# Reordering the opening of a fused retention and feed-forward kernel, with three units' outputs unfused and the last product split over two PSUM banks

## The chip, the core and the metric

The kernel runs on one core of a Trainium2 chip. The metric is the device time of one execution in microseconds (us); the figure given for a kernel is the median over its runs. TensorE (PE) does the matrix products, VectorE (DVE), ScalarE (ACT) and GpSimd (POOL) work beside it, each in the order of its own program; SyncE (SP), ScalarE and GpSimd also issue DMA transfers. The engines meet through semaphores. PSUM, where TensorE writes its results, has eight banks of 2 KB per partition.

## The reference

Multi-head retention (8 batches, 8 heads, 576 positions, head width 64) is followed by a two-layer feed-forward block over the 4608 resulting tokens:

```
scores = q @ k.T / 8                       # per batch and head, 576 x 576
ret    = scores * D                        # D[i,j] = gamma_h ** (i-j) for i >= j, else 0
x      = (ret @ v), heads side by side     # 4608 x 512
h      = x @ w_in                          # 512 -> 2048
g      = max(0.01 * h, h)                  # leaky ReLU
out    = g @ w_out                         # 2048 -> 512
```

Inputs and output are fp32; the kernel computes its products in fp16 with fp32 accumulation.

## The kernel before

**Retention by chunks.** The 4608 tokens are cut into 36 units of 128 tokens, each of two chunks of 64 tokens. Nine chunks make up one batch entry, so a unit can straddle two entries. Within a chunk the product q k^T v is done with a triangular mask; everything earlier in the entry comes through a running state, a 64 x 64 matrix for each head. The powers of gamma are folded into q and v by a table (`decay`), and the state is rescaled every four chunks.

For a unit u the steps are these; the names are those of the code.

- `load(u)` brings q, k and v (256 KB each) to SBUF. `cast_k`, `cast_q`, `cast_v` turn them into fp16; the last two also multiply by the table. For units 0 to 7 q and v are cast on VectorE and k on ScalarE.
- `transpose_pe(u, x)` turns k (x = 1) or q (x = 0) on TensorE into a PSUM bank, and `transposed` copies it out. From unit 8 on a DMA transposes instead (`transpose_dma`, issued on SP); `ahead(u)` issues the casts and that transpose.
- `scores(u)` is 32 matmuls into two PSUM banks: k^T q for both chunks, and each chunk's own contribution to the state.
- `state(u, j)` adds that contribution to the running state (VectorE; two operations where it is rescaled), `state_cast` makes an fp16 copy, `masks(u)` applies the triangle.
- `outputs(u)` is 32 matmuls that leave two separate parts in PSUM: what comes from the unit's own chunks and what comes from the state. `own(u)` (ScalarE) copies the first part to SBUF, and `add(u)` (VectorE) adds the second to it and writes x. `outputs_acc(u)` lets TensorE add both parts in PSUM, in two rounds with a drain between them, and `x_copy(u)` (ScalarE) writes x.

**Feed-forward by groups.** Four units make a group of 512 tokens. The first layer is computed in pieces: `h_half` (two blocks of 128 hidden features over two units), `h_unit` (four blocks over one unit), `h_block` (one block over a whole group); each is followed by a leaky ReLU on ScalarE (`leaky`, L387) into `gt`. `halves(g, (a, fb), ...)` calls `h_half` for token half a and feature pair fb. The second layer of group 0 is the plain product (`wide`); from group 1 on each group's second layer is done with seven half-size products in place of eight (`seven`), whose sums of inputs are prepared by `mix` and `mix_weights` on VectorE. `keep`, `give` and `store` combine the products and send them out. In the last group the final product p7 is added in two parts, so that each part can be stored by itself.

**PSUM.** The pool `sc` holds one buffer of two banks for scores, `ot` one buffer of two banks for outputs, and `acc` four single banks that rotate through everything else: turns, warm-up products, h pieces, second-layer products.

**What sets the order.** The order is written out by hand (`manual_schedule`): each engine runs its instructions in program order. Lines 560 to 621 are the opening, in which units 0 to 3 are done one after the other while the first weights arrive; `keep_warm(n)` puts n matmuls on zeros on TensorE there (L551). Lines 691 to 759 weave units 4 to 7 and the first-layer pieces of groups 0 and 1. `turn(u, x)` is a turn whose copy is on VectorE; `settle(u)` is state, cast, mask, state; `finish(u)` is `outputs_acc`, `x_copy` and a state cast on ScalarE; `finish2(u)` is `outputs`, `own`, `add`. Lines 766 to 798 hold the steady part.

The loads of the opening go out on three queues: SP has k of unit 0, half of q of unit 0, and k of unit 1; ScalarE's queue has two tables of constants and the other half of q of unit 0; GpSimd's queue has v of unit 0, then everything else of units 1 to 7 and all weights. The first layer's weights come in quarters of the hidden features, each in two transfers.

Of the kernel before, what the change touches and what calls it, by code (L numbers as in the profile page):

```python
# [9 lines left out]
FP = mybir.dt.float32  # L10
# [8 lines left out]
def kernel(  # L19
# [186 lines left out]
    def transposed(u, x, copy):  # L206
        copy(out=qkT[u][:, x], in_=tr[u, x])  # L207

    def scores(u):
        a = sc_pool.tile([P, 2, 2, NP, CH], FP, name="sc")  # L210
        sc_tiles[u] = a
# [96 lines left out]

    def outputs_acc(u):

        ot = ot_pool.tile([P, 2, 2 * NP, CH], FP, name="ot")
        ot_tiles[u] = ot
# [139 lines left out]
    def g_part(g, a, b):  # L452
        return g_t[g][:, b * HF : (b + 1) * HF, a * HT : (a + 1) * HT]
# [15 lines left out]
    def seven(g, hooks, last=False):  # L469
# [3 lines left out]

        def product(name, lhs, rhs, fresh):
            if fresh:
                r[name] = acc_pool.tile([P, 2, HN], FP, name="acc")
            order = (
                [(f, tb) for tb in range(2) for f in range(HF)]
                if last
                else [(f, tb) for f in range(HF) for tb in range(2)]  # L480
            )
            for n, (f, tb) in enumerate(order):
                nc.tensor.matmul(  # L483
                    out=r[name][:, tb, :],
                    lhsT=lhs[:, f, tb * P : (tb + 1) * P],
                    rhs=rhs[:, f, :],
                    start=fresh and n == 0,
                    stop=f == HF - 1,
                    skip_group_check=True,
                )  # L490

        def keep(name, of, plus=None):
            r[name] = m_pool.tile([P, 2, HN], FP, name=name)
            if plus is None:
                nc.scalar.copy(out=r[name], in_=r[of])
            else:
                nc.vector.tensor_tensor(out=r[name], in0=r[of], in1=r[plus], op=ADD)

        def give(a, b, of, plus=None, parts=1):
            if ("o", a) not in r:  # L500
                r["o", a] = o_pool.tile([P, 2, DM], FP, name="osb")
            for n in range(parts):
                ts = slice(n * 2 // parts, (n + 1) * 2 // parts)
                to = r["o", a][:, ts, b * HN : (b + 1) * HN]
                if plus is None:
                    nc.scalar.copy(out=to, in_=r[of][:, ts])
                else:
                    nc.vector.tensor_tensor(  # L508
                        out=to, in0=r[of][:, ts], in1=r[plus][:, ts], op=ADD
                    )  # L510
# [9 lines left out]
            if r["n", a] == 2 and not (last and a == 1):  # L520
# [8 lines left out]
            ("p5", g_part(g, 0, 0), w_part(1, 1), False, lambda: give(0, 1, "p5", "u2")),  # L529
            (  # L530
                "p7", g_part(g, 1, 1), w_mix[:, 3], False,
                lambda: give(1, 0, "p7", "u2", 2 if last else 1),
            ),
        )
# [25 lines left out]
    keep_warm(7)  # L560
    load(0, {1: nc.sync, 0: (nc.sync, nc.scalar), 2: nc.gpsimd})
    load(1, {1: nc.sync, 0: nc.gpsimd, 2: nc.gpsimd})
# [11 lines left out]


    cast_k(0)
    transpose_pe(0, 1)
    transposed(0, 1, act_copy)
    keep_warm(3)
    cast_q(0, nc.vector)  # L580
    cast_v(0, nc.vector)
    transpose_pe(0, 0)
    transposed(0, 0, act_copy)
    keep_warm(3)
    cast_k(1)
    for u in range(4):
        n = u + 1
        scores(u)
        if not u:
            keep_warm(3)  # L590
        state(u, 0)
        state_cast(u, dve_copy, (0,))
        masks(u)
        if not u:
            cast_q(1, nc.vector)
            cast_v(1, nc.vector)
        state(u, 1)
        if n < 4:
            transpose_pe(n, 1)
            transposed(n, 1, act_copy)  # L600
            if not u:
                keep_warm(3)
                outputs_acc(0)
                x_copy(0)
                keep_warm(1)
            transpose_pe(n, 0)
            transposed(n, 0, act_copy)
            keep_warm(3 if u else 2)
        if n < 3:
            cast_k(n + 1)  # L610
            cast_q(n + 1, nc.vector)
            cast_v(n + 1, nc.vector)
        if u < 3:
            state_cast(u, act_copy, (1,))
        if u == 1:
            outputs_acc(1)
            x_copy(1)
            keep_warm(2)
        elif u == 2:
            outputs_acc(2)  # L620
            x_copy(2)

# [67 lines left out]

    halves(0, (0, 0), (0, 1))
    finish2(3)
    state_cast(3, act_copy, (1,))
    halves(0, (0, 2), (0, 3), (1, 0))
    cast_k(4)
    cast_qv(4)
    halves(0, (1, 1))
    turn(4, 1)
# [17 lines left out]
    cast_k(6)  # L716
    cast_qv(6)
    halves(0, (0, 6), (0, 7))
    finish(5)
    halves(0, (1, 6))  # L720
# [3 lines left out]
    turn(6, 0)  # L724
    cast_qv(7)
    h_unit(5, 0)
    scores(6)
    settle(6)
    h_unit(5, 1)
    turn(7, 1)  # L730
    halves(1, (0, 4))
    finish(6)
    turn(7, 0)
    halves(1, (0, 5))
    scores(7)
    settle(7)
    load(8, after=(w_out_loads[2],))
    load(9)
    halves(1, (0, 6), (0, 7))
    h_unit(6, 0)  # L740
    finish(7)
    h_unit(6, 1)
    mix_weights(0, 0)
# [9 lines left out]
    mix_weights(2, 1)  # L753
    halves(1, (1, 5), (1, 6))
    load(11)
    ahead(9)
    mix_weights(3, 0)
# [71 lines left out]
```

## Time and profile before

| | |
|---|---|
| median of 7 runs | 294.23 us (291.59 to 295.34) |
| the profiled execution | 291.83 us |
| its span, first to last instruction | 290.1 us |
| TensorE busy, matmuls | 281.0 us (97%) |
| VectorE, ScalarE, GpSimd busy | 170.5, 144.3, 104.1 us |
| first h matmul (L373) starts | 19.11 us |
| warm-up matmuls (L551) | 30, busy 9.6 us |

The profile is of one execution. Its rows name the line, the engine, the operation, the tile that is written and the tiles that are read, with the number of instructions and their duration; in square brackets stands how long the engine had been idle before and what released it. Times in the timeline count from the span's start. Matmuls are pipelined: several overlap, so that a row's duration is longer than the distance between two starts. The time outside the span, 1.7 us in this execution, belongs to the measured time too.

### The profile page before, as it was taken

How to read it: one execution, taken by the hardware profiler on the slowest of the kernel's cores; microseconds unless marked ns; L12 is line 12 of the kernel's file. 1: busy time of each engine (PE TensorE's matmuls, PEld its weight loads, DVE VectorE, ACT ScalarE, POOL GpSimd, SP SyncE). 2: the span in 40 equal slices, each digit the busy share in tenths (PEclk: the TensorE clock that was granted, in tenths of full speed). 3: DMA queues.
4: the chain of work that ended last, by engine and by line, in shares of the span. 5: the costliest groups of instructions: out<-in, count | busy, mean ns of one | idle time of the engine just before them, and what ended most of it. 6: DMA issues, size and time to landing. Idle time of an engine off the chain costs nothing.

```text
span 290.1 us, 9449 instructions
## 1 busy us (share of the span) xinstructions
PE 281.0 (97%) x4118; PEld 191.2 (66%) x4118; DVE 170.5 (59%) x293; ACT 144.3 (50%) x254; POOL 104.1 (36%) x124
## 2 busy tenths in 40 slices
PE   6899999999999999999999999999999999999994
PEld 2468888745874587458745874588448844874583
DVE  1874577964762596359635862686268636841342
ACT  3666766724327732773277317731773176317510
POOL 8869601753433225222524342234225413000000
PEclk9999999999999999999999999999999999999999
DMA  7999999998999986966797669889986151012003
GB/s 199 303 226 198 295 206 208 224 231 177 239 217 293 210 186 156 280 149 147 159 251 174 148 147 277 159 127 168 272 167 144 42 180 38 5 66 81 0 2 145
DMA packets 131738, 50.01 MB, mean 172 GB/s; under 512 B 121264, under 2 KB 126000, under 8 KB 131696
## 3 DMA queue, kind: packets, MB, share of 16 engines
q1 hardware_dynamic: 124864, 39.46, 59.3%
q0 software_dynamic: 6016, 9.70, 14.9%
q8 instruction: 32, 0.52, 0.8%
q10 hardware_dynamic: 816, 0.24, 0.3%
q14 instruction: 10, 0.08, 0.1%
HBM read 36.81 MB, written 9.44 MB: 159 GB/s over the span
## 4 chain that ended last, share of the span: by engine, by line
PE 91%; DVE 3%; DMA 2%; ACT 1%; issue 1%; SPq 0%; DVEq 0%
PE acc L373 43%; PE acc L483 34%; PE acc L423 5%; PE sc L215 3%; DMA t<-in_k_dram 2%; PE ot L291 2%; PE sc L224 1%; PE ot L302 1%; PE ot L321 1%; PE acc L200 1%; DVE s L233 1%; ACT qkT L207 1%; PE ot L333 0%; ACT qk L172 0%; PE acc L551 0%
## 5 line engine op out<-in xcount | busy, mean ns | idle before, releaser
L373 PE MATMUL acc<-xT,w_in 128*128 128x512 f16 (+2 forms) x768 | 130.9, 326 | 0.0
L387 ACT ACTIVATE gt<-acc 128x512 f16<-128x512 f32 x144 | 85.9, 597 | 57.0 <-PE acc L373 55.5
L373 PEld LDWEIGHTS <-w_in 128*128 128x128 f16 x768 | 68.0, 98 | 51.5
L483 PEld LDWEIGHTS <-gt 128*128 128x128 f16 x640 | 61.7, 97 | 9.3
L233 DVE TENSOR_TENSOR s<-sc,cs 128x512 f16<-128x512 f32 x36 | 24.7, 686 | 40.8 <-PE sc L224 40.8
L273 POOL CAST st<-s 128x512 f16<-128x512 f32 x21 | 12.8, 609 | 93.5 <-DVE s L257 57.9
L483 PE MATMUL acc<-w_out,gt 128*128 128x256 f16 x384 | 45.9, 273 | 0.2
L355 ACT COPY own<-ot 128x512 f32<-128x512 f32 x30 | 17.6, 585 | 42.8 <-PE ot L302 35.2
L175 POOL TENSOR_TENSOR qk<-t,cs 128x512 f16<-128x512 f32 x28 | 30.4, 1087 | 15.7 <-ACT gt L387 14.5
L467 DVE TENSOR_TENSOR mix<-gt 128x1024 f16<-128x1024 f16 x16 | 14.7, 916 | 29.0 <-ACT gt L387 29.0
L179 POOL TENSOR_TENSOR v<-t,cs 128x512 f16<-128x512 f32 x28 | 31.3, 1118 | 0.5 <-PE acc L373 0.5
L483 PE MATMUL acc<-w_mix,gt 128*128 128x256 f16 x256 | 30.6, 273 | 0.0
L483 PE MATMUL acc<-w_mix,mix 128*128 128x256 f16 x256 | 29.5, 273 | 0.0
L483 PEld LDWEIGHTS <-mix 128*128 128x128 f16 x256 | 24.9, 98 | 3.2 <-DVE mix L467 0.2
L172 ACT CAST qk<-t 128x512 f16<-128x512 f32 x36 | 22.3, 620 | 1.8 <-DMA t<-in_k_dram 1.8
L360 DVE TENSOR_TENSOR xT<-ot,own 128x512 f16<-128x512 f32 x30 | 20.5, 683 | 3.0 <-ACT own L355 3.0
L257 DVE TENSOR_TENSOR s<-sc,s 128x256 f32<-128x256 f32 x40 | 16.8, 419 | 3.6 <-PE sc L224 3.1
L508 DVE TENSOR_TENSOR osb<-acc,u 128x512 f32<-128x512 f32 (+1 forms) x17 | 11.1, 656 | 8.0 <-PE acc L483 8.0
L215 PEld LDWEIGHTS <-qkT 64*64 64x64 f16 x576 | 7.7, 107 | 11.2 <-issue 9.7
L276 POOL CAST st<-s 128x256 f16<-128x256 f32 x7 | 3.2, 453 | 32.2 <-DVE s L261 20.3
L423 PE MATMUL acc<-w_out,gt 128*128 128x512 f16 x64 | 14.3, 380 | 0.0
L467 DVE TENSOR_TENSOR mix<-mix,gt 128x1024 f16<-128x1024 f16 x16 | 14.0, 879 | 0.5
(52 smaller groups left out, 238.4 us busy)
## 6 DMA issues: line engine op xcount, KB each, us to landing
out_dram<-osb SPq DMA_DIRECT2D x17, 512.0 KB, 3.8
t<-in_k_dram SPq DMA_DIRECT2D x27, 256.0 KB, 4.0
t<-in_q_dram SPq DMA_DIRECT2D x25, 256.0 KB, 4.5
t<-in_v_dram SPq DMA_DIRECT2D x25, 256.0 KB, 4.9
w_in<-in_moe_w_in_dram POOLq DMA_DIRECT2D x8, 256.0 KB, 7.3
w_out<-in_moe_w_out_dram POOLq DMA_DIRECT2D x4, 512.0 KB, 10.2
t<-in_v_dram POOLq DMA_DIRECT2D x7, 256.0 KB, 6.7
t<-in_q_dram POOLq DMA_DIRECT2D x6, 256.0 KB, 6.5
```

Source lines behind the costliest of these rows:

```text
L172: nc.scalar.copy(out=qk16[u][:, 1], in_=t32[u, 1])
L175: eng.tensor_tensor(out=qk16[u][:, 0], in0=t32[u, 0], in1=decay(u, 0), op=MUL)
L179: eng.tensor_tensor(out=v16[u], in0=t32[u, 2], in1=decay(u, 1), op=MUL)
L233: nc.vector.tensor_tensor(out=s16s[u], in0=sc_tiles[u][:, :, 0], in1=mask_sb.unsqueeze(1).unsqueeze(1).to_broadcast([P, 2, NP, CH]), op=MUL,)
L257: nc.vector.tensor_tensor(out=to, in0=st, in1=carry[0], op=ADD)
L355: nc.scalar.copy(out=owns[u], in_=ot_tiles[u][:, :, 0:NP].rearrange("q j c t -> q c j t"))
L360: nc.vector.tensor_tensor(out=x_of(u).rearrange("q (c g) t -> q c g t", g=2), in0=ot_tiles[u][:, :, NP : 2 * NP].rearrange("q g (c j) t -> ...
L373: nc.tensor.matmul(out=hps[:, n, :], lhsT=w_in16[:, c, f * P : (f + 1) * P], rhs=xT[g][:, c, ts], start=(c == 0), stop=(c == NP - 1),)
L387: nc.scalar.activation(out=out, in_=in_, func=mybir.ActivationFunctionType.Lrelu)
L423: nc.tensor.matmul(out=ys[tb], lhsT=g_t[0][:, f, tb * P : (tb + 1) * P], rhs=w_out16[:, f, :], start=(f == 0), stop=(f == NF - 1),)
L467: nc.vector.tensor_tensor(out=z[:, fs], in0=a[:, fs], in1=b[:, fs], op=op)
L483: nc.tensor.matmul(out=r[name][:, tb, :], lhsT=lhs[:, f, tb * P : (tb + 1) * P], rhs=rhs[:, f, :], start=fresh and n == 0, stop=f == HF - ...
```

## The change

**Opening.** It is written out step by step. Unit 0's q is loaded whole on SP's queue. The scores of units 0 and 2 go to the two banks of `ot` instead of those of `sc`, and the outputs of units 0 to 2 go to one bank of `acc`, so that the scores of unit u + 1 can be issued ahead of the outputs of unit u. The warm-up products are 23 instead of 30. The first h piece, `h_half(0, 0, 0)`, stands ahead of `masks(2)` and `scores(3)`.

**After the opening.** `cast_k(4)` and `cast_qv(4)` stand ahead of the h piece (1, 0).

**Units 5 to 7.** They use `outputs`, `own` and `add` in place of `outputs_acc` and `x_copy`. `cast_v(6)` moves behind the sum of unit 5, the casts of q and v of unit 7 move behind `settle(6)`, the sum of unit 6 moves behind the turn of unit 7's q, and unit 7's outputs move ahead of the h pieces (0, 6) and (0, 7) of group 1, which in turn move behind both `h_unit(6, ...)`. `ahead(9)` is issued before `load(11)`.

**The last product.** In the last group p7 lies in two banks, one for each half of its tokens, and each use of it is added and stored in two parts.

```diff
-    def scores(u):
-        a = sc_pool.tile([P, 2, 2, NP, CH], FP, name="sc")
+    def scores(u, pool=None):
+        if pool is None:
+            a = sc_pool.tile([P, 2, 2, NP, CH], FP, name="sc")
+        else:
+            a = pool.tile([P, 2, 2, NP, CH], FP, name="ot")
...
-    def outputs_acc(u):
-
-        ot = ot_pool.tile([P, 2, 2 * NP, CH], FP, name="ot")
+    def outputs_acc(u, pool=None):
+
+        if pool is None:
+            ot = ot_pool.tile([P, 2, 2 * NP, CH], FP, name="ot")
+        else:
+            ot = pool.tile([P, 1, 2 * NP, CH], FP, name="acc")
...
         def product(name, lhs, rhs, fresh):
+            apart = last and name == "p7"
             if fresh:
-                r[name] = acc_pool.tile([P, 2, HN], FP, name="acc")
+                r[name] = [
+                    acc_pool.tile([P, 1 if apart else 2, HN], FP, name="acc")
+                    for _ in range(2 if apart else 1)
+                ]
...
                 nc.tensor.matmul(
-                    out=r[name][:, tb, :],
+                    out=r[name][tb][:, 0, :] if apart else r[name][0][:, tb, :],
...
-                    start=fresh and n == 0,
+                    start=fresh and (f == 0 if apart else n == 0),
...
-        def give(a, b, of, plus=None, parts=1):
+        def give(a, b, of, plus=None):
+            parts = len(r[of])
...
                     nc.vector.tensor_tensor(
-                        out=to, in0=r[of][:, ts], in1=r[plus][:, ts], op=ADD
+                        out=to, in0=r[of][n], in1=r[plus][:, ts], op=ADD
                     )
...
-    load(0, {1: nc.sync, 0: (nc.sync, nc.scalar), 2: nc.gpsimd})
+    load(0, {1: nc.sync, 0: nc.sync, 2: nc.gpsimd})
...
+    def turn_act(u, x):
+        transpose_pe(u, x)
+        transposed(u, x, act_copy)
+
+    def state_first(u):
+        state(u, 0)
+        state_cast(u, dve_copy, (0,))
+
+    def state_last(u):
+        state(u, 1)
+        state_cast(u, act_copy, (1,))
+
+    def first_outputs(u):
+        outputs_acc(u, acc_pool)
+        x_copy(u)
+
     cast_k(0)
-    transpose_pe(0, 1)
-    transposed(0, 1, act_copy)
+    turn_act(0, 1)
     keep_warm(3)
     cast_q(0, nc.vector)
     cast_v(0, nc.vector)
-    transpose_pe(0, 0)
-    transposed(0, 0, act_copy)
+    turn_act(0, 0)
     keep_warm(3)
     cast_k(1)
-    for u in range(4):
...
+    cast_q(1, nc.vector)
+    scores(0, ot_pool)
+    keep_warm(2)
+    state_first(0)
+    turn_act(1, 1)
+    turn_act(1, 0)
+    keep_warm(2)
+    cast_v(1, nc.vector)
+    masks(0)
+    cast_k(2)
+    scores(1)
+    turn_act(2, 1)
+    keep_warm(2)
+    state_last(0)
+    first_outputs(0)
+    state_first(1)
+    cast_q(2, nc.vector)
+    cast_v(2, nc.vector)
+    turn_act(2, 0)
+    keep_warm(2)
+    cast_k(3)
+    masks(1)
+    scores(2, ot_pool)
+    turn_act(3, 1)
+    keep_warm(2)
+    state_last(1)
+    first_outputs(1)
+    state_first(2)
+    cast_q(3, nc.vector)
+    cast_v(3, nc.vector)
+    turn_act(3, 0)
+    h_half(0, 0, 0)
+    masks(2)
+    scores(3)
+    state_last(2)
+    first_outputs(2)
+    state_first(3)
+    masks(3)
+    state(3, 1)
...
-    halves(0, (0, 0), (0, 1))
+    halves(0, (0, 1))
     finish2(3)
     state_cast(3, act_copy, (1,))
-    halves(0, (0, 2), (0, 3), (1, 0))
+    halves(0, (0, 2), (0, 3))
     cast_k(4)
     cast_qv(4)
-    halves(0, (1, 1))
+    halves(0, (1, 0), (1, 1))
...
     cast_k(6)
-    cast_qv(6)
+    cast_q(6, nc.vector)
     halves(0, (0, 6), (0, 7))
-    finish(5)
+    finish2(5)
+    cast_v(6, nc.vector)
+    state_cast(5, act_copy, (1,))
     halves(0, (1, 6))
     turn(6, 1)
     cast_k(7)
     halves(0, (1, 7))
     turn(6, 0)
-    cast_qv(7)
     h_unit(5, 0)
     scores(6)
     settle(6)
+    cast_qv(7)
     h_unit(5, 1)
     turn(7, 1)
     halves(1, (0, 4))
-    finish(6)
+    outputs(6)
+    own(6)
     turn(7, 0)
+    add(6)
+    state_cast(6, act_copy, (1,))
     halves(1, (0, 5))
     scores(7)
     settle(7)
     load(8, after=(w_out_loads[2],))
     load(9)
+    h_unit(6, 0)
+    h_unit(6, 1)
+    finish2(7)
+    state_cast(7, act_copy, (1,))
     halves(1, (0, 6), (0, 7))
-    h_unit(6, 0)
-    finish(7)
-    h_unit(6, 1)
     mix_weights(0, 0)
...
+    ahead(9)
     load(11)
-    ahead(9)
```

More of the change, by code (lines that the diff above doesn't have):

```diff
@@ L494, in keep @@
             if plus is None:
-                nc.scalar.copy(out=r[name], in_=r[of])
+                nc.scalar.copy(out=r[name], in_=r[of][0])
             else:
-                nc.vector.tensor_tensor(out=r[name], in0=r[of], in1=r[plus], op=ADD)
-        def give(a, b, of, plus=None, parts=1):
+                nc.vector.tensor_tensor(out=r[name], in0=r[of][0], in1=r[plus], op=ADD)
+        def give(a, b, of, plus=None):
+            parts = len(r[of])
             if ("o", a) not in r:
@@ L505, in give @@
                 if plus is None:
-                    nc.scalar.copy(out=to, in_=r[of][:, ts])
+                    nc.scalar.copy(out=to, in_=r[of][n])
                 else:
                     nc.vector.tensor_tensor(
-                        out=to, in0=r[of][:, ts], in1=r[plus][:, ts], op=ADD
+                        out=to, in0=r[of][n], in1=r[plus][:, ts], op=ADD
                     )
@@ L529, in seven @@
             ("p5", g_part(g, 0, 0), w_part(1, 1), False, lambda: give(0, 1, "p5", "u2")),
[L530 to L533, printed above, removed]
+            ("p7", g_part(g, 1, 1), w_mix[:, 3], False, lambda: give(1, 0, "p7", "u2")),
         )
@@ L581 @@
     cast_v(0, nc.vector)
-    transpose_pe(0, 0)
-    transposed(0, 0, act_copy)
+    turn_act(0, 0)
     keep_warm(3)
     cast_k(1)
-    for u in range(4):
[L587 to L621, printed above, removed]
+    cast_q(1, nc.vector)
[37 more added lines that the diff above has]
+    state(3, 1)
     def halves(g, *items):
```

## The prediction

> **What bounds the kernel now.** I read the page first (busy shares, slices, granted clock), then busy time by stage, then the timeline of the stages the diff touches, then the DMA queues in half-microsecond windows.
>
> ```profile
> span 290.1 us, 9449 instructions
> PE 281.0 (97%) x4118; PEld 191.2 (66%) x4118; DVE 170.5 (59%) x293; ACT 144.3 (50%) x254; POOL 104.1 (36%) x124
> PEclk9999999999999999999999999999999999999999
> ```
>
> Then busy time by stage:
>
> ```profile
> 10.00:15.00 5.00, 4.46 (x94) 2.58 (x91) 4.61 (x11) 3.94 (x8) 3.59 (x7) 1.00 1.13 272
> 20.00:25.00 5.00, 5.00 (x74) 4.05 (x71) 3.24 (x6) 3.98 (x8) 4.80 (x7) 1.00 0.85 135
> 40.00:45.00 5.00, 4.85 (x115) 4.24 (x113) 4.21 (x10) 2.77 (x6) 0.00 (x0) 1.00 1.22 204
> ```
>
> These lines give PE, PEld, DVE, ACT and POOL busy time, clock, DMA share, GB/s. From 20 us on TensorE is full but for some tenths of a microsecond: there only TensorE time removed, or one of its waits removed, counts. Before 20 us it waits for data and fills in with warm-up matmuls (L551). The timeline of the opening:
>
> ```profile
> 8.94 0.62 ACT L172 CAST qk<-t 128x512 f16<-128x512 f32 x1 [1.01 <-DMA t<-in_k_dram]
> ...
> 16.80 0.81 PE L551 MATMUL acc<-idle 128*128 128x512 f16 x3
> ...
> 17.64 0.68 POOL L132 DMA_DIRECT2D t<-in_v_dram  x1 [0.57 <-DMA w_in<-in_moe_w_in_dram]
> 17.89 0.31 PE L321 MATMUL ot<-s,v 64*64 64x64 f16 x8 [0.27 <-ACT qkT L207]
> ...
> 19.11 1.16 PE L373 MATMUL acc<-xT,w_in 128*128 128x256 f16 x9
> ```
>
> k of unit 1 lands at 8.9 and starts everything; the second half of the first w_in quarter lands at about 17.4 (POOL's next issue is released at 17.64 by it); the first h matmul runs at 19.11, outputs(2) and scores(3) in between. Later, and at the end:
>
> ```profile
> 25.33 0.40 PE L200 MATMUL acc<-ident,qk 128*128 128x128 f16 x4 [0.32 <-ACT qk L172]
> ...
> 29.85 0.32 PE L291 MATMUL ot<-s,v 64*64 64x64 f16 x16
> ...
> 30.23 1.92 PE L373 MATMUL acc<-xT,w_in 128*128 128x256 f16 x16
> ...
> 36.54 0.31 PE L321 MATMUL ot<-s,v 64*64 64x64 f16 x8
> ...
> 37.44 1.05 PE L373 MATMUL acc<-xT,w_in 128*128 128x256 f16 x8
> ...
> 286.17 0.76 DVE L508 TENSOR_TENSOR osb<-acc,u 128x256 f32<-128x256 f32 x2 [1.05 <-PE acc L483]
> 286.63 0.84 SPq L513 DMA_DIRECT2D out_dram<-osb  x2
> ```
>
> A plain outputs call costs TensorE 30.23 - 29.85 = 0.38 us, an accumulating one 37.44 - 36.54 = 0.90 us. The last two adds start together, after the last matmul.
>
> **What the Trainium skill says.** "DMA: Bandwidth & Descriptors", section "Issuing engines are not separate DMA queues": loads issued from several engines interleave on the same 16 engines, and a second queue saves only issue time. The trace agrees: from 4.0 to 5.0 us ACT's queue moves 0.10 MB (half of q) and SP's about 0.02; from 5.0 k of unit 1 follows on SP. "TensorE: Matmul & The Clock Gate", Part 1: after an idle window of about 3.4 us TensorE runs at half clock. The first seven warm-ups take 3.12/7 = 0.446 us each, later ones 0.81/3; no idle in the opening exceeds the 1.36 us before 6.91, and the clock row never falls. "PSUM — Partial Sum Buffer", section on bank collisions: guard PSUM by bank, not by address. The 286.17 row agrees: half the last product was complete eight matmuls earlier, about 0.9 us, and its add still waited.
>
> **Opening.** Gone: 7 of 30 warm-ups (nothing useful), half of q on ACT's queue. Moved: scores of units 0 and 2 to ot's banks, outputs 0 to 2 to an acc bank; the work itself stays. Walk on ACT, which the new order loads most: cast_k1 8.94, copies of both turns of unit 1 to 11.1, cast_k2 to 11.65, copy of unit 2's k to 12.7, state cast 13.1, x_copy(0) behind outputs(0) (TensorE 12.35) to 13.75, copy of unit 2's q to 14.3, cast_k3 14.9, its copy 15.9, state cast 16.25, x_copy(1) to 17.06. VectorE in step: masks(1) ends 14.3, cast_q3 16.4, cast_v3 17.0, masks(2) 17.6. So x is ready 0.35 us before w_in at 17.4, and the first h half starts near 17.5, held by w_in. From there both versions owe the same: two h halves (0.88 each), scores(3) 0.38, outputs_acc(2) 0.85, outputs(3) 0.38: 3.4 us. So outputs(3) ends at 20.9 instead of 21.34: **gain 0.45**. masks(3) ends 20.2, needed 20.5. Waiting h is new on TensorE: behind it stand scores(3) and outputs(2), which VectorE then waits for; it is the 0.6 us idle from 16.9 that was warm-ups.
> q of unit 0 in one queue: SP's k of unit 1 now has 128 KB more ahead of it on SP. Same bytes, same order as the half-microsecond windows show them moving, so I take 0. Upper bound: SP moved 0.26 MB from 5.0 to 8.5 beside POOL, 75 GB/s, so 128 KB costs 1.7 us, less 0.35 slack: a loss of 1.35 against 17.5. Lower bound: 0.5 earlier, worth nothing as w_in decides.
>
> **cast_k(4)** moves ahead of one leaky on ACT: k of unit 4 landed at 20.8, the cast ends near 23 for a turn at 25. **Gain 0.32**, the wait in the 25.33 row. h half (1,0) moves behind it; x(3) is ready near 22.5, needed 22.7.
>
> **Units 5 to 7.** Removed from TensorE: 3 x (0.90 - 0.38) = 1.56, and 0.24 at 43.0 to 43.24, where outputs(6) waited for masks(6) behind two casts of unit 7 (1.19 us). Added: an add of 0.69 on VectorE each; own (0.58) replaces x_copy on ACT. Walk, with TensorE's outputs(5) at 36.54 as before: h half 0.88, turn 0.22, half, turn, h_unit 0.89 lead to scores(6) at 40.01. own(5) and add(5) end 38.55, cast_v6 39.16: hidden under these 3.1 us. settle(6) runs 40.52 to 42.58 (2.06 from its first start to the next operation's, as 41.38 to 43.44 shows); cast_q7 to 43.26, cast_v7, the copy of k7 43.78, of q7 44.12 to 44.53, add(6) to 45.15. TensorE reaches the end of outputs(6) at 42.76 and then **waits 0.55** for cast_q7 (turn(7,0); behind it stands h half (1,0,5)), 0.18 for q7's copy, 0.22 for add(6). h_unit(6,0) starts 45.2, outputs(7) ends 47.36; own(7) and add(7) end 48.8, hidden by two h halves until 49.12. h_unit(7,1) ends 50.9 against 52.0: **gain 1.1**. cast_v(6), state_cast(6) and finish2(7) only change place inside this walk.
>
> **ahead(9) before load(11).** On SP its transpose passes three loads: 1.9 us earlier; they come some 1.6 to 2 us later, so cast_k(11) on ACT waits till about 61.1; behind it there the next copy is due near 62: nothing. POOL's casts keep their order. The mixes start 1.5 us later on VectorE, so masks(8) comes near 61.3 and sc is free at 62.3; scores(9) is due near 63. Cost 0, and 0.5 if POOL's sharing stretches them further.
>
> **The last product.** First half added at 285.3 under the matmuls; the second add and its store start at 286.17 and 286.63 instead of 286.55 and 287.07: **gain 0.44**. One add of 0.69 becomes two of 0.42 and one store two, 0.37 each, all before 285: hidden. Of four acc banks the second bank of p7 is the fifth taken; it reuses p1's, copied out by 279.8.
>
> **Sum:** 0.45 + 0.32 + 1.1 + 0.44 = 2.3 us. The profiled execution took 291.83 (span 290.1 and 1.7 around it), so 289.5. The median of the seven runs is 294.23, 2.4 above it, so I forecast 294.2 - 2.3 = **292.0**.
>
> **Rivals.**
> 1. VectorE keeps up (its queue order hides less than I read into it, or w_in lands earlier): the 0.95 of new waits shrinks to 0.2 and the opening gives 0.6. Gain 3.2: 291.0. For: every wait in my walk is under 0.6 us. Against: cast_q7 stands in order behind settle(6).
> 2. A wait takes the place of the one removed: k of unit 1 late by the upper bound (opening -1.35), or add and casts so late that units 5 to 7 give nothing. Gain 0.5 to 1.2: about 293.3. For: ACT works 7.3 of the 8.7 us from 8.9 to 17.6. Against: the order of bytes is the same.
> 3. Slower: the clock falls. With fewer warm-ups and the idle before h, TensorE drops to half clock as h begins. One window of 3.4 us at half clock loses 1.7 us; from 1.35 windows on the kernel is slower than before, with two it ends at 295.3, with three at 297. For: warm-ups go from 30 to 23. Against: no idle in my walk reaches 0.8 us, and before survived 1.36.
>
> **Chances.** Forecast 0.48, own range 291.2 to 292.9; rival 1 0.27; rival 2 0.16; rival 3 0.09. One per cent, 2.9 us, is about what a measurement of this kernel can tell from no change (its runs spread from 291.6 to 295.3). Faster by over 1% needs under 291.3: most of rival 1 and some of the forecast, 0.33. Slower by over 1% needs over 297.2: the worst of rival 3 and spread, 0.07. Within: 0.60. The range leaves out the best of rival 1 and rival 3: 290.0 to 294.0.
>
> **What would show it.** First h matmul at 17.4 to 17.7 right after w_in, with x_copy(1) done; outputs(3) ending near 20.9; no wait before turn(4,1); one L291/L302 group each for units 5 to 7, a wait of about half a microsecond before turn(7,0); h_unit(7,1) ending 1.9 us earlier than before; the last store issued 0.4 us after the last matmul. Wrong if k of unit 1 lands after 9.3, if the clock row falls, or if scores(9) waits for masks(8).

## The result, and the profile after

| | kernel before | kernel after |
|---|---|---|
| median, us (executions) | 293.12 (31) | 289.61 (12) |
| lowest to highest, us | 291.42 to 295.46 | 288.38 to 291.29 |
| profiled execution, us (span) | 291.83 (290.1) | 291.29 (289.5) |

The measured ratio is 0.9881, with a 95% interval of 0.9849 to 0.9913; between the medians the gain is 3.5 us. I had forecast 292.0, in a range of 290.0 to 294.0: the direction was right, the gain larger than I allowed. The ratios of this document leave out executions more than 1.5% above the fastest of their kernel (none here, 11 of 112 of the kernel before further down, 2 of 14 of one experiment); the medians keep them, and none would move by more than 0.4 us without them. The profiled execution of the kernel after is the longest of its twelve, and one thing in it is not typical: the clock row (`PEclk`, the clock that TensorE was granted, in tenths of full speed) shows a 7 where the kernel before has a 9:

```profile
span 289.5 us, 9432 instructions
PE 279.5 (97%) x4111; PEld 190.8 (66%) x4111; DVE 171.8 (59%) x297; ACT 143.8 (50%) x254; POOL 104.6 (36%) x124
PEclk9979999999999999999999999999999999999999
```

Busy time by stage, kernel after (the columns are PE, PEld, DVE, ACT, POOL, granted clock, DMA share, GB/s):

```profile
15.00:20.00 5.00, 3.94 (x84) 2.53 (x84) 2.61 (x6) 2.45 (x5) 2.00 (x3) 0.77 1.08 249
20.00:25.00 5.00, 4.91 (x99) 4.14 (x94) 3.76 (x8) 3.50 (x9) 4.59 (x7) 0.89 0.79 125
```

Of the ten microseconds from 15 to 25, 1.15 + 0.55 = 1.7 us of clock are missing. From 18 to 21 us the clock is 0.50, so this is some 3.4 us at half speed; such a stretch is called a lost window below. It begins with the first h matmuls. Timeline of the kernel after (start, duration, engine, line, operation, idle time before and what ended it), the opening:

```profile
16.36 0.59 ACT L347 CAST xT<-acc 128x512 f16<-128x512 f32 x1 [0.43 <-PE acc L339]
...
17.62 1.86 PE L379 MATMUL acc<-xT,w_in 128*128 128x256 f16 x8 [0.97 <-DMA w_in<-in_moe_w_in_dram]
...
21.13 1.05 PE L379 MATMUL acc<-xT,w_in 128*128 128x256 f16 x8
22.10 0.32 PE L294 MATMUL ot<-s,v 64*64 64x64 f16 x16
22.48 3.67 PE L379 MATMUL acc<-xT,w_in 128*128 128x256 f16 x32
25.98 0.39 PE L200 MATMUL acc<-ident,qk 128*128 128x128 f16 x4
```

The first half of h takes 1.86 us and the second 1.05, for the same eight matmuls. Still, in this execution the step is as predicted: x_copy(1) ends at 16.95, h waits for w_in, and starts at 17.62.

Units 5 to 7 and the end, in the timeline of the kernel after:

```profile
37.19 0.32 PE L294 MATMUL ot<-s,v 64*64 64x64 f16 x16
37.57 1.05 PE L379 MATMUL acc<-xT,w_in 128*128 128x256 f16 x8
...
44.06 0.40 PE L200 MATMUL acc<-ident,qk 128*128 128x128 f16 x4 [0.39 <-DVE qk L175]
...
285.86 0.42 DVE L519 TENSOR_TENSOR osb<-acc,u 128x256 f32<-128x256 f32 x1 [0.45 <-PE acc L493]
```

Outputs of unit 5 cost 0.38 us in place of 0.90; turn(7,0) has its new wait of 0.39 (foreseen 0.55); of the last product only a half is still to be added when the matmuls end at 285.82. From the start of outputs(5) to the first matmul of the second layer (L429, L423 in the kernel before) it takes 18.03 us (37.19 to 55.22), against 18.99 (36.54 to 55.53): 0.96 gained.

### The profile page after: what moved, and what is told of

The parts are those of the page before. It is cut to its first block, busy times and chain, and to the rows that moved or that the text cites. A ratio compares the mean times of both kernels' runs of the same rounds, so it can differ in the third digit from the quotient of the medians.

```text
span 289.5 us, 9432 instructions
## 1 busy us (share of the span) xinstructions
PE 279.5 (97%) x4111; PEld 190.8 (66%) x4111; DVE 171.8 (59%) x297; ACT 143.8 (50%) x254; POOL 104.6 (36%) x124
## 4 chain that ended last, share of the span: by engine, by line
PE 90%; POOL 3%; DMA 3%; DVE 3%; issue 0%; POOLq 0%
PE acc L379 43%; PE acc L493 34%; PE acc L429 5%; POOL t L132 3%; PE sc L218 3%; DMA w_in<-in_moe_w_in_dram 3%; PE ot L294 2%; PE ot L305 1%; PE sc L227 1%; PE acc L200 0%; DVE s L236 0%; DVE xT L366 0%; DVE stmp L263 0%; DVE s L264 0%; DVE qkT L207 0%
## 5 line engine op out<-in xcount | busy, mean ns | idle before, releaser
L236 DVE TENSOR_TENSOR s<-sc,cs 128x512 f16<-128x512 f32 x34 | 23.3, 686 | 38.9 <-PE sc L227 38.9
L361 ACT COPY own<-ot 128x512 f32<-128x512 f32 x33 | 19.3, 585 | 42.8 <-PE ot L305 35.5
L179 POOL TENSOR_TENSOR v<-t,cs 128x512 f16<-128x512 f32 x28 | 31.9, 1139 | 0.0
L473 DVE TENSOR_TENSOR mix<-gt 128x1024 f16<-128x1024 f16 x16 | 14.0, 878 | 28.8 <-ACT gt L393 28.8
L366 DVE TENSOR_TENSOR xT<-ot,own 128x512 f16<-128x512 f32 x33 | 22.5, 683 | 5.5 <-ACT own L361 5.5
L260 DVE TENSOR_TENSOR s<-sc,s 128x256 f32<-128x256 f32 x37 | 15.5, 419 | 4.0 <-PE sc L227 3.3
L429 PE MATMUL acc<-w_out,gt 128*128 128x512 f16 x64 | 14.3, 379 | 0.0
L473 DVE TENSOR_TENSOR mix<-mix,gt 128x1024 f16<-128x1024 f16 x16 | 13.1, 826 | 0.5
```

Source lines behind the costliest of these rows:

```text
L179: eng.tensor_tensor(out=v16[u], in0=t32[u, 2], in1=decay(u, 1), op=MUL)
L236: nc.vector.tensor_tensor(out=s16s[u], in0=sc_tiles[u][:, :, 0], in1=mask_sb.unsqueeze(1).unsqueeze(1).to_broadcast([P, 2, NP, CH]), op=MUL,)
L361: nc.scalar.copy(out=owns[u], in_=ot_tiles[u][:, :, 0:NP].rearrange("q j c t -> q c j t"))
L366: nc.vector.tensor_tensor(out=x_of(u).rearrange("q (c g) t -> q c g t", g=2), in0=ot_tiles[u][:, :, NP : 2 * NP].rearrange("q g (c j) t -> ...
L429: nc.tensor.matmul(out=ys[tb], lhsT=g_t[0][:, f, tb * P : (tb + 1) * P], rhs=w_out16[:, f, :], start=(f == 0), stop=(f == NF - 1),)
L473: nc.vector.tensor_tensor(out=z[:, fs], in0=a[:, fs], in1=b[:, fs], op=op)
```

## The experiments

Every execution reports its mean granted clock. A loss of 1.7 us of clock over 290 us leaves 0.994, and the values fall into two groups, 0.994 and below and 0.997 and above; with 0.9955 as the border, those above it are called full-clock executions here. The 31 executions of the kernel before in the table above have no clock on record, so the three series that were taken beside the experiments stand in for them:

| kernel | below 0.9955 | their median, us | median of the others | all |
|---|---|---|---|---|
| before, first series | 15 of 37 | 293.56 | 291.80 | 292.38 |
| before, second series | 15 of 32 | 294.52 | 291.58 | 293.15 |
| before, third series | 19 of 43 | 294.13 | 291.95 | 293.12 |
| after | 1 of 12 | 291.29 | 289.48 | 289.61 |
| new opening alone | 0 of 8 | - | 290.70 | 290.70 |
| units 5 to 7 and the order of ahead(9) alone | 10 of 22 | 292.93 | 290.52 | 291.86 |
| last product in two banks alone | 8 of 14 | 294.08 | 291.85 | 293.19 |
| before, unit 0's q in one queue | 0 of 22 | - | 291.40 | 291.40 |
| before, five more warm-ups | 0 of 14 | - | 291.98 | 291.98 |
| after, unit 0's q in two queues | 7 of 19 | 291.05 | 289.68 | 290.25 |
| after, four warm-ups before h | 1 of 6 | 291.09 | 289.62 | 289.63 |
| after, unit 7's q cast earlier | 0 of 4 | - | 289.07 | 289.07 |
| after, w_in ahead of unit 3's loads | 4 of 20 | 292.51 | 290.69 | 290.93 |
| after, warm-ups in both gaps, q of unit 7 earlier | 0 of 6 | - | 289.54 | 289.54 |

Every one of the 49 executions of the kernel before under 0.9955 took 293.0 us or more. Nine of its 63 full-clock executions did so too, up to 296.6; what made those long isn't shown. Full-clock medians of the same kernel differ by up to 0.4 us between the series, so a difference of that size between two series says nothing.

The theory at first was that of the prediction: its parts add up, and h is held by w_in. The rival was its third, the clock, which could gain as well as lose.

**The new opening alone**, with cast_k(4), units 5 to 7 and the tail as before:

```diff
-    load(0, {1: nc.sync, 0: (nc.sync, nc.scalar), 2: nc.gpsimd})
+    load(0, {1: nc.sync, 0: nc.sync, 2: nc.gpsimd})
...
+    scores(0, ot_pool)
...
+    h_half(0, 0, 0)
...
-    halves(0, (0, 0), (0, 1))
+    halves(0, (0, 1))
```

> The kernel before with the new opening alone (q of unit 0 in one queue, scores of units 0 and 2 in the banks of ot, outputs of units 0 to 2 in an acc bank, first h piece ahead of scores(3)); the rest as before. Theory A, the missing gain lies in the opening, whose first h matmul now follows w_in at once instead of a chain of casts and turns: 1.0 to 1.8 us faster than before. Rival B, the opening gives the 0.45 us of the walk and the rest lies elsewhere: 0.2 to 0.6 faster.

Ratio 0.9932 (0.9904 to 0.9961), 2 us of the gain and more than either theory had; 1.1 us between full-clock medians, and none of the 8 executions lost clock, against 15 of 37 of the kernel before. In its trace the first h matmul ran at 16.91 without a wait, as w_in and x came earlier in this execution, and turn(4,1) still waits:

```profile
24.36 0.40 PE L200 MATMUL acc<-ident,qk 128*128 128x128 f16 x4 [0.32 <-ACT qk L172]
```

From the start of outputs(3) to that turn it takes 4.36 us (4.37 in the kernel before), in the kernel after 22.10 to 25.98, 3.88: cast_k(4) gives 0.49. The idle time was 0.32; the rest is that turn(4,1) now overlaps the drain of the last h matmul (32 of them last 3.67 us, and the next operation starts 3.50 after their first). Later, with the old order of load(11) and ahead(9), scores(9) waits for a transpose; the chain of waits of this kernel has

```profile
58.10 5.84 DMA qkT<-qk
63.99 0.32 PE sc L218 x16
```

where in the kernel before TensorE was late enough. The opening's lead ahead of it was 0.96 us (first L429 at 54.57 against 55.53), at scores(9) it is 0.75 (63.99 against 64.74), and at the end of the span 0.6. So 0.2 is lost at scores(9), where the old order holds a faster opening back; the rest isn't traced. With the new order nothing is lost there: the kernel after with four warm-ups before h, told below, starts L429 at 53.51 (2.0 us of lead) and ends its span at 287.8 (2.3, of which the last product gives 0.3).

**Units 5 to 7 and ahead(9) alone** on the kernel before:

```diff
-    cast_qv(6)
+    cast_q(6, nc.vector)
...
-    finish(5)
+    finish2(5)
+    cast_v(6, nc.vector)
+    state_cast(5, act_copy, (1,))
...
+    ahead(9)
     load(11)
-    ahead(9)
```

> The kernel before with the new order from cast_k(6) on alone: plain outputs with a sum on VectorE for units 5 to 7, and ahead(9) before load(11). Theory A: the 1.0 to 1.1 us of the walk. Rival B, part of the missing gain lies here: 1.6 to 2.0 us, all TensorE time that is removed, with the three new waits gone in most executions.

Ratio 0.9966 (0.9941 to 0.9992), 1.0 us, as theory A had it; 10 of 22 executions lose clock, so that this part doesn't touch the loss. outputs(5) to L423 takes 36.21 to 54.24, the same 18.03 as in the kernel after.

**The last product in two banks alone**, on the kernel before:

```diff
+            apart = last and name == "p7"
...
-                r[name] = acc_pool.tile([P, 2, HN], FP, name="acc")
+                r[name] = [
+                    acc_pool.tile([P, 1 if apart else 2, HN], FP, name="acc")
+                    for _ in range(2 if apart else 1)
+                ]
```

> The kernel before with p7 of the last group in two banks alone. Both theories: 0.3 to 0.5 us faster, the last store issued about 0.45 us after the last matmul instead of 0.9. If the last store's landing grows by what it gains, 0.0 to 0.2.

Ratio 1.001 (0.9978 to 1.0042): no gain that can be measured. The trace has one, smaller than predicted: from the end of the last matmul to the end of the span 3.68 us (286.72 to 290.4), against 3.96 (286.14 to 290.1). The last store's issue ends 0.5 us earlier behind the matmul, yet the span ends only 0.28 earlier: the rest lies between the end of the issue and the end of the span, where the store lands.

**Four warm-ups in the idle time before h**, on the kernel after:

```diff
+    keep_warm(4)
     h_half(0, 0, 0)
```

> The changed kernel with four warm-up matmuls ahead of the first h piece, in the idle time of about 0.7 us in which it waits for w_in. If the fall of the clock there (granted mean 0.994 in the profile after, h piece of 1.8 us instead of 0.9) is common, this is 0.3 to 1.0 us faster than the changed kernel and its clock 1.000; if it is rare or not caused by that idle time, it is the same or up to 0.5 slower.

289.63 us, as the kernel after. Its trace shows full clock at h and a span of 287.8, 1.7 us less than the profiled execution above. A second comparison is closer: the kernel with unit 7's q cast earlier, told below, is the same up to there, waits as long for w_in, and keeps its clock.

```profile
17.58 1.03 PE L379 MATMUL acc<-xT,w_in 128*128 128x256 f16 x8 [1.06 <-DMA w_in<-in_moe_w_in_dram]
...
20.67 0.32 PE L294 MATMUL ot<-s,v 64*64 64x64 f16 x16
```

From the first h matmul to outputs(3) it takes 3.09 us, and 4.48 in the profiled execution (17.62 to 22.10): the lost window costs 1.4 us up to there. But it was 1 execution in 12, and here 1 in 6. That is too few to tell whether these warm-ups do anything, and too rare to be what the median is about.

**The kernel before, unchanged, in two more traces.** If the clock matters, it shows in the kernel that loses it.

> The kernel before, once more, for its trace: in 15 of 37 of its executions the mean granted clock was under 0.9955, and those took 1.8 us longer at the median (293.56 against 291.80). If such an execution is caught, theory A (the matmul clock is lost in the opening) has one stretch of some 3.4 us at about half clock somewhere between 4.5 and 22 us, most likely starting near 7 to 9 us, behind the 1.36 us in which TensorE waits for unit 0's q; the rest of the trace shifts by 1.4 to 1.8 us. Theory B (the longer executions are late for another reason, a late load say, and the clock is a by-product) has the shift ahead of the half-clock stretch. With no half clock the span is 290.1 again.

> A second look at the kernel before, with the expectation of the first: a half-clock stretch in 4 of 10 looks.

Both executions lost a window (spans 292.2 and 291.5, against 290.1). The timeline that I had predicted from has, around unit 0's q,

```profile
6.16 0.69 DVE L175 TENSOR_TENSOR qk<-t,cs 128x512 f16<-128x512 f32 x1 [4.87 <-DMA t<-in_q_dram]
...
6.91 0.40 PE L200 MATMUL acc<-ident,qk 128*128 128x128 f16 x4 [1.36 <-DVE qk L175]
```

The first of the two has

```profile
7.41 0.69 DVE L175 TENSOR_TENSOR qk<-t,cs 128x512 f16<-128x512 f32 x1 [6.13 <-DMA t<-in_q_dram]
...
8.16 0.40 PE L200 MATMUL acc<-ident,qk 128*128 128x128 f16 x4 [1.97 <-DVE qk L175]
8.40 0.81 PE L551 MATMUL acc<-idle 128*128 128x512 f16 x3
...
9.61 1.29 PE L551 MATMUL acc<-idle 128*128 128x512 f16 x3
```

and this busy time by stage (clock in the third column from the end):

```profile
8.00:10.00 2.00, 1.81 (x41) 1.13 (x42) 0.97 (x3) 1.10 (x2) 2.00 (x4) 0.96 1.06 352
10.00:12.00 2.00, 2.00 (x10) 0.88 (x7) 1.97 (x5) 0.59 (x1) 2.00 (x5) 0.50 1.01 334
12.00:14.00 2.00, 1.91 (x32) 1.09 (x31) 1.82 (x4) 0.41 (x1) 1.97 (x3) 0.69 1.17 221
```

The second has

```profile
7.43 0.47 PE L200 MATMUL acc<-ident,qk 128*128 128x128 f16 x4 [2.12 <-DVE qk L175]
```

TensorE stands 1.97 and 2.12 us before turn(0,0), in place of 1.36. From the clock column it then runs 3.4 us at half clock: from about 9.8 to 13.2 in the first, where 1.7 us of work at full clock lie between the wait and this stretch, and from about 7.6 to 11.0 in the second. There are two costs, the late turn and the half clock; together h starts at 21.22 and 20.51 in place of 19.11. The half clock alone is less than the 1.7 us of clock that it takes away: from turn(0,0) to the first h matmul it takes 13.06 and 13.08 us here, and 11.52, 11.83 and 12.20 in three full-clock traces of this opening (units 5 to 7 alone, last product alone, the kernel before). That is 0.9 to 1.6 us. What TensorE waits for is VectorE's cast of unit 0's q, which starts at 7.41 (6.68 in the second, 6.16 before), released by q's load. Where that load is late can be seen in the DMA queues. The first of the two traces, from 4.0 to 4.5 us and from 5.0 to 7.0 us (queue, packets, MB, share of time; q1 is SP's, q10 ScalarE's, q0 GpSimd's):

```profile
q0 software_dynamic: 14, 0.06, 61.0%
q10 hardware_dynamic: 242, 0.06, 53.3%
...
q0 software_dynamic: 115, 0.38, 52.5%
q1 hardware_dynamic: 936, 0.24, 52.4%
q10 hardware_dynamic: 96, 0.02, 5.3%
```

Most of q's half goes through ScalarE's queue by 4.5 us, while SP's queue moves nothing; its last 96 packets, 0.02 MB, trickle between 5 and 7 us among 936 of SP's and 115 large ones of GpSimd's. The cast starts at 7.41, behind the last of them.

**Five more warm-ups in that wait**, on the kernel before, q's load left as it was:

```diff
     transposed(0, 1, act_copy)
-    keep_warm(3)
+    keep_warm(8)
```

> The kernel before with 8 warm-up matmuls in place of 3 behind unit 0's first turn, so that the 1.36 us wait for unit 0's q at 5.5 us falls to about 0.2 us; nothing else is moved. Theory A (the old opening loses a window of the clock in 4 of 10 executions, because of the idle TensorE around 5.5 to 8.5 us): executions under 0.9955 fall from 40% to under 15%, and the median falls by 0.7 to 1.2 us (ratio 0.996 to 0.9975), to the 291.8 of the full-clock executions. Theory C (the lost window has another place, at the start of h or in unit 1 to 3's gaps): the share stays at 30 to 50% and the ratio within 0.999 to 1.001. Theory D (warm-ups delay the turn): 0.1 to 0.3 us slower.

None of 14 executions lost clock, and the median fell to 291.98, near that of the full-clock executions of the kernel before (291.58 to 291.95). The ratio is 0.9974 (0.9941 to 1.0006): about 0.8 us, 1.2 between the medians, and the interval just includes 1. But 0 of 14 against 15 of 32 in the same series doesn't look like chance. In the trace q is no earlier than before (its cast starts at 6.38), and only the idle time is shorter:

```profile
7.13 0.40 PE L200 MATMUL acc<-ident,qk 128*128 128x128 f16 x4 [0.44 <-DVE qk L175]
```

So theory A has its place and its cause: it is TensorE's idle time here that loses the clock.

**Unit 0's q in one queue, alone**, on the kernel before:

```diff
-    load(0, {1: nc.sync, 0: (nc.sync, nc.scalar), 2: nc.gpsimd})
+    load(0, {1: nc.sync, 0: nc.sync, 2: nc.gpsimd})
```

> The kernel before with one part of the change alone: q of unit 0 whole on SP's queue. Theory A (the half of q on ScalarE's queue lands late, VectorE's first cast starts at 6.2 to 7.4 us and TensorE stands idle 1.4 to 2.1 us, long enough to lose a clock window in 4 of 10 executions): the cast starts at 5.8 to 6.0 in its trace, executions under 0.9955 fall from 45% to under 15%, and the median falls by 0.8 to 1.5 us (ratio 0.997 to 0.995). The prediction's step (0, a loss of up to 1.35 as bound): ratio 1.000, or up to 1.0046 if k of unit 1 behind it is late.

Ratio 0.9945 (0.9923 to 0.9968): 1.6 us, 1.7 between the medians. The part that I had put at nothing is the largest of all on its own. No execution of 22 lost clock, against 19 of 43, and against the full-clock ones of the kernel before (291.95) it is still 0.56 faster. Its trace has

```profile
6.11 0.69 DVE L175 TENSOR_TENSOR qk<-t,cs 128x512 f16<-128x512 f32 x1 [4.82 <-DMA t<-in_q_dram]
...
6.86 0.40 PE L200 MATMUL acc<-ident,qk 128*128 128x128 f16 x4 [0.84 <-DVE qk L175]
```

and the same two stretches of its DMA queues are

```profile
q1 hardware_dynamic: 337, 0.08, 74.4%
q0 software_dynamic: 22, 0.09, 71.7%
...
q1 hardware_dynamic: 1013, 0.26, 56.5%
q0 software_dynamic: 116, 0.38, 52.2%
```

q's second half now fills the time from 4.0 to 4.5 us in which SP's queue had been empty. Whether some of q's packets still come late can't be counted, as k of unit 1 follows in the same queue. And k of unit 1 is not delayed: its cast starts at 7.77 (8.94 in the profiled execution of the kernel before, 9.08 and 8.42 in the two further ones). The cast of q starts at 6.2 to 7.4 us in the seven traces with q split and at 5.8 to 6.8 in the seven with q in one queue: earlier by and large, with an overlap.

**The reverse: q back in two queues in the kernel after.**

```diff
-    load(0, {1: nc.sync, 0: nc.sync, 2: nc.gpsimd})
+    load(0, {1: nc.sync, 0: (nc.sync, nc.scalar), 2: nc.gpsimd})
```

> The kernel after with the one part of its opening undone that touches the first loads: q of unit 0 split again over SP's and ScalarE's queues. The prediction's step put this at 0, with +1.35 us as a bound for a loss from one queue. If one queue is what lets the clock hold (theory A with q as cause), executions under 0.9955 come back at 30 to 50% and the median rises by 0.7 to 1.2 us to about 290.5. If it is neutral, 289.5 with few such executions; if one queue costs time as the bound had it, this is faster by up to 0.5 us.

7 of 19 executions lose clock again (1 of 12 without), median 290.25 against 289.61; between the full-clock ones (289.68 and 289.48) no difference is shown. Those counts alone are few, but over all kernels here 6 of 78 executions with q in one queue lost clock, and 74 of 167 with q split and three warm-ups behind unit 0's first turn. So it is q's queue that keeps the clock, and not the new order of the opening. By medians q's queue is worth 1.7 us on the old opening and 0.6 on the new, the latter between two series and without an interval of its own. The parts don't add up. That in the new opening w_in holds the first h matmul, or nearly so, and hides a part of what comes ahead of it, would fit; it wasn't tested.

**w_in first.** On the kernel after, the first quarter of w_in ahead of unit 3's loads, two h halves ahead of its turns:

```diff
-    load(3, nc.gpsimd)
     load_w_in(0)
+    load(3, nc.gpsimd)
...
+    h_half(0, 0, 0)
     cast_q(3, nc.vector)
+    turn_act(3, 1)
...
+    h_half(0, 0, 1)
+    turn_act(3, 0)
```

> The kernel after with the first quarter of w_in ahead of unit 3's loads in GpSimd's queue, and the first two h halves ahead of unit 3's turns. If w_in's landing at 17.5 us is what holds the first h matmul, as the prediction has it, w_in lands some 3 us earlier and h starts as soon as x_copy(1) has its x (near 17.0): 0.4 us earlier, unless unit 3's loads, now 3 us later, hold its turns, which then stand before outputs(3): 0.5 to 1.5 us slower. The likelier of the two: slower by about 0.5, so 290.1.

Slower than the kernel after by 1.2 us among full-clock executions, more than the half microsecond expected. In its trace h no longer waits for w_in but for x, and unit 3, now late, brings waits of 0.2, 0.5 and 0.4 us. The wait before turn(0,0), and the last two of these:

```profile
7.59 0.61 PE L200 MATMUL acc<-ident,qk 128*128 128x128 f16 x4 [2.10 <-DVE qk L175]
...
23.63 0.32 PE L294 MATMUL ot<-s,v 64*64 64x64 f16 x16 [0.52 <-DVE s L236]
...
25.50 0.71 PE L379 MATMUL acc<-xT,w_in 128*128 128x256 f16 x5 [0.44 <-DVE xT L366]
```

So moving w_in ahead of unit 3's loads gains nothing in this order: unit 3 is then waited for. How far w_in binds h in the kernel after this trace can't say, as it lost a window ahead of h (at half clock from about 7.4 to 10.8 us). This kernel, with q in one queue and the same loads ahead of it as the kernel after, still lost clock in 4 of 20 executions; in its trace the cast of q starts at 6.84 and TensorE stands 2.10 us before turn(0,0). So one queue doesn't rule out a late q.

**Unit 7's q cast earlier**, to take the new wait of 0.39 away:

```diff
-    settle(6)
-    cast_qv(7)
+    state(6, 0)
+    state_cast(6, dve_copy, (0,))
+    masks(6)
+    cast_q(7, nc.vector)
+    state(6, 1)
+    cast_v(7, nc.vector)
```

> The kernel after with VectorE's cast of unit 7's q put between masks(6) and the second state of unit 6, so that turn(7,0) finds its input. The prediction's walk of units 5 to 7 (a new wait before turn(7,0), 0.39 us in the trace after) expects that wait gone and the state's casts and add(6) late by the 0.69 of the cast at most: 0.2 to 0.4 us faster than the kernel after (289.6), so 289.2. If VectorE just moves the wait, the idle time shows before h_unit(6,0) (0.15 us now) and the time stays 289.6.

289.07 in four executions, not separable from 289.48. The trace decides: the wait has moved.

```profile
43.93 0.32 PE L218 MATMUL sc<-qkT 64*64 64x64 f16 x16 [0.32 <-DVE qkT L207]
44.53 1.95 PE L379 MATMUL acc<-xT,w_in 128*128 128x128 f16 x32 [0.15 <-DVE xT L366]
```

From outputs(6) to h_unit(6,0) it takes 41.83 to 44.53, 2.70 us; in the kernel after 43.23 to 45.92, 2.69. So VectorE's whole queue up to add(6) seems to decide, not the order within it.

**All of it together** on the kernel after: unit 7's q cast as above, and

```diff
     turn_act(0, 1)
-    keep_warm(3)
+    keep_warm(7)
...
+    keep_warm(4)
     h_half(0, 0, 0)
```

> The kernel after with what the runs point to: 7 warm-up matmuls in place of 3 behind unit 0's first turn and 4 ahead of the first h half, so that no idle stretch of TensorE in the opening is over 0.5 us, and unit 7's q cast early. No execution under 0.9955, and the full-clock median of the kernel after (289.48) less 0.3 for the wait: 289.2, ratio 0.987 to 0.989.

289.54 (ratio 0.9882, 0.983 to 0.9933), no lost clock in six executions, and no faster than the kernel after, where 289.2 was expected: the wait of unit 7's q only moves, as above, and the median of the kernel after is hardly touched by its one execution in twelve.

## Why the prediction was off

**The step that failed is the last one: "The median of the seven runs is 294.23, 2.4 above it, so I forecast 294.2 - 2.3".** The forecast of 292.0 lies 2.4 us above the measured 289.61. Of these, 1.1 are the base, as the median of all 31 executions of the kernel before is 293.12 and not 294.23; 1.3 are the gain, 3.5 us and not 2.2. I carried the 2.4 us between the profiled execution and the median over as if the change couldn't touch them. They were no constant: the seven times were 291.6, 291.7, 293.3, 294.2, 295.0, 295.2 and 295.3, two groups, and my profile (291.83) came from the lower one. The clocks of these seven are not on record; in the three series, 49 of the 58 executions of 293.0 us or more had lost a window, so most of the upper group will have. The lost window is what the change nearly abolishes.

The sum itself, 2.3 us, is about what full-clock executions gained: 2.1 to 2.5, from 291.58, 291.80 or 291.95 to 289.48. In part this is luck, as the terms below show.

**"q of unit 0 in one queue ... I take 0", with a loss of 1.35 as the upper bound and a gain excluded "as w_in decides".** The sign was wrong, and it is the part behind the failed step. I read that 0.10 MB of q passed through ScalarE's queue from 4.0 to 5.0 us, and took the last packets of it, between 5 and 6 us, for nothing:

```profile
q10 hardware_dynamic: 27, 0.01, 2.9%
```

VectorE's cast starts behind them, at 6.16. The 1.35 assumed that SP's queue was full ahead of unit 1's k; from 4.0 to 5.0 us it was nearly empty, with about 0.01 MB moved. And the exclusion held only for the path through w_in, not for the clock. The Trainium skill, in "DMA: Bandwidth & Descriptors", section "Issuing engines are not separate DMA queues", says that a second queue saves only issue time. The runs go against that: here the choice of the queue changed when q's cast could start, and was worth 1.6 us (ratio 0.9945).

**Rival 3 had the right mechanism and the wrong sign.** I priced a half-clock window at 1.7 us. That is the clock it takes away; the time was 0.9 to 1.6 us in the old opening and 1.4 in the new one up to outputs(3). The medians of the executions with lost clock are 1.8 to 2.9 above those without, with the late load and, in those near 0.988, perhaps a second window in it. But I let it count only against the new kernel, for its fewer warm-ups, with "before survived 1.36". One execution had survived it; in the three series 49 of 112 lost clock, and the new one, with seven warm-ups fewer, loses a window in 1 of 12. The Trainium skill, in "TensorE: Matmul & The Clock Gate", Part 1, gives the idle time that loses the clock as a window of about 3.4 us; it says too that the window runs free, so that how many matmuls run at the low clock varies from run to run. The second agrees with the runs, in which one kernel loses the clock in some executions and not in others, and the stretches of half clock do last 3.4 us. The first doesn't bound a gap, as I had read it: of the 14 traces, the three with the longest waits before turn(0,0) (1.97, 2.10 and 2.12 us) lost a window there, and the others, up to 1.87 us (the kernel after with q split), did not. And before h the profiled execution of the kernel after lost one behind 0.97 us, where a wait of 1.06 in another trace did not.

**Opening, 0.45:** outputs(3) starts at 20.00, 20.31, 20.40 and 20.67 in the four full-clock traces of the new opening with q in one queue, against 20.96 in the profile that I used: 0.29 to 0.96. The range holds the 0.45, and single traces can't say more: two other full-clock traces of the old opening have 20.63 and 21.04, the old opening with q in one queue has 20.53, with nothing but five more warm-ups 20.50, and the new one with q split 20.25. The mechanism is as written in two traces, with h held by w_in until 17.62 and 17.58; in the trace of the new opening alone h starts at 16.91 without a wait.

**cast_k(4), 0.32:** 0.49, through the drain that is overlapped. **Units 5 to 7, 1.1:** 0.96, with the waits where the walk had them, but shorter (0.39 for 0.55, 0.15 for 0.22). That the gain nearly fits is luck: the terms named there (1.56 + 0.24 gained, 0.95 of waits) make 0.85 and not 1.1, and the walk's steps are too short (3.09 us from the end of outputs(5) to scores(6), where both traces have 3.19). **Last product, 0.44:** 0.28 in the trace; the landing of the store takes part of it back. **ahead(9), 0:** no wait of scores(9) appears, as said, and cast_k(11) waits as said; but the old order would have cost a faster opening at least 0.2 us, which I hadn't seen.

These four, and 0.29 to 0.96 of the opening, make 2.0 to 2.7 by the traces, against 2.1 to 2.5 between full-clock medians; the rest of the 3.5 us, about 1.2, is what the lost windows add to the median of the kernel before.

## What to carry to other kernels

Look at the spread of the times before trusting one profile: if they form two groups, ask which one the profile came from and what the other waits for, since a change to the first loads can be worth more there than on the path that the profile shows. In the DMA view look for the last packet of a load, not for the bulk: here a load split over two queues was as late as the slower of them. And an idle stretch of TensorE in the opening can cost a lost window on top of its own length; a few warm-up matmuls in it, where nothing waits behind them, are cheap cover (five of them took the loss from 15 of 32 executions to 0 of 14).

## What was not expected of the hardware

- In the first of the two further traces of the kernel before, a load of 128 KB in small packets on ScalarE's queue had most of its bytes through by 4.5 us and its last 12 packets between 6 and 7 us, beside GpSimd's large packets and SP's. Why the last packets come so late isn't shown.
- SP's queue moved nearly nothing of unit 1's k, issued at 1.9 us, before 5.0 us in the traces with q split (0.00 to 0.02 MB from 4.0 to 5.0), and its cast was no later with q's second half ahead of it (7.6 to 8.7 us, against 8.3 to 9.1). Why the queue is idle there isn't shown.
- The busy share of TensorE ahead of a lost window isn't one number. In the 3.4 us ahead of it TensorE was busy 47% (6.4 to 9.8 us) and 38% (4.2 to 7.6) in the two further traces of the kernel before, but 70% in the kernel after (14.1 to 17.5); and a stretch with 44% (5.2 to 8.6, chosen around the wait) in the kernel after with q split went without loss. Ahead of the 70% case most matmuls were 64x64; whether those count less wasn't tried.
